# Attention masks on one Trainium2 core: the step between groups of 64 keys moved into idle rows of the query and key images, and the first mask product of a set cut from 128 keys to 64

## Chip, core and metric

The kernel runs on one core of one Trainium2 chip. The metric is the device time of one execution in microseconds; the number that counts is the median of several executions. The engines are named as in the profile: PE is TensorE (PEld are its weight loads), DVE is VectorE, ACT is ScalarE, POOL is GpSimd, SP is the SyncE queue that issues most of the transfers.

## What is computed

Two attention blocks read the same x (2048 rows of 512) and are mixed row by row by a gate. Block A works in four segments of 512 rows with 32 heads of 16: inside a segment it is causal softmax attention, and a memory of the earlier segments is added to it. Block B is full attention over all 2048 rows. Cut to what matters here:

```python
def _A_ref(x, wq, wk, wv, wo, beta):        # H=32 heads, Dh=16, N=4 segments, L=512
    ar = jnp.arange(L)
    mask = (ar[:, None] < ar[None, :]) * (-1e9)
    for s in range(N):
        qs, ks, vs = q[:, :, s], k[:, :, s], v[:, :, s]
        logits = jnp.einsum("bhqd,bhkd->bhqk", qs, ks) * scale + mask
        p = _softmax(logits, axis=-1)
        a_dot = jnp.einsum("bhqk,bhkd->bhqd", p, vs)
        a_mem = num / den                     # phi(q) against the memory M, z
        outs.append(g * a_mem + (1.0 - g) * a_dot)
        M, z = M + phi(k)^T v, z + sum(phi(k))
    return o @ wo

def _B_ref(x, wqkv, wo):                      # H=32, full attention over S=2048
    p = _softmax(jnp.einsum("bhqd,bhkd->bhqk", q, k) * (Dh ** -0.5))
    return o @ wo

g = sigmoid((x * gate_w).sum(-1))
return g * a + (1 - g) * b
```

The mask is the part that the change touches: a query sees the keys up to and including its own place in the segment.

## The kernel before

**Images.** Queries and keys of a unit are kept as images of 128 partitions: two halves of 64 rows (j = 0 and 1), one head in each half, and two heads behind one another (p = 0 and 1). Of the 64 rows of a half, 48 hold the 16 numbers of a head as high and low parts, in an order that makes one product over 64 rows the full-precision score. Rows 48 and 49 hold the negated row maximum on the query side (two parts, written by `m_rows`) and ones on the key side. Rows 50 to 63 are zero in all images: these are the idle rows. `load_qk` fetches an image from device memory; for a query image it writes rows 0 to 49 (the last two with zeros), for a key image rows 0 to 47. So what stands in rows 50 to 63 is written once, before the first unit, and stays. A's images are KA and QA (two buffers each), B's are KB and QB (three each).

**Units.** A unit is four heads times 512 queries. There are 32 of A (u = 0 to 31, causal, 512 keys) and 32 of B (u = 32 to 63, 2048 keys). After the projections the main loop runs k from 0 to 31; step k takes B's unit 32 + k in 32 groups (n = 0 to 31) and then A's unit k in 5 groups (n = 32 to 36). A group is laid down in PE's order by hand: `t_group` makes transposed scores of two heads in two PSUM banks and ACT turns them into exponentials; then come the maximum tasks that the table `plan` gives for this place; then `pvs` multiplies earlier exponentials with the values.

**Maxima.** The exponentials need the row maximum of every query beforehand. It is made one unit ahead, from a second score product that is not transposed (queries on partitions): `s_b` for B and `s_a` for A write into one of two buffers `SBK` of two banks each, and DVE reduces the buffer to a maximum. In step k the six calls of `s_a` for unit k + 1 stand at n = 32, 33, 34, 34, 35 and 36 (`ST_A`: the query blocks of 128 numbered 3, 3, 2, 2, then 1 and 0 with both p in one call). That stretch of a step, n = 32 to 36, is called the A stage below.

**The mask in `s_a`.** For query block i the score product covers the keys 0 to 128(i + 1). The last 128 keys of it are the diagonal block, on which a mask is accumulated in the same bank. It takes two more products for each half j, each over 64 rows in bf16: `crows[r, n2 - 1]` picks 64 of the 128 queries, and `cmask[r, n2 - 1]` holds, for each of them, -4e9 at the keys behind it. With n2 = 1, the first 64 queries, all 128 keys of the diagonal block are covered (keys 64 to 127 lie behind all of these queries); with n2 = 2, the last 64 queries, only the last 64 keys. The two halves j run beside each other on different rows of the array. So a set (one i and one p) has six products: two scores, two first mask products of 128 columns, two second ones of 64 columns; a unit has 8 sets, and 4 first products in each call for blocks 1 and 0, which hold two sets.

In the transposed scores of `t_group` the mask is applied later: POOL sets the entries behind the diagonal to zero after the exponential (`affine_select`).

**Before the main loop.** `constants` fills small tables on DVE and POOL in the first 14 us. `set_aux` copies 16 rows of constants (ones in the first two and zeros, or zeros alone) into rows 48 to 63 of an image, with two transfers that POOL issues; the list `ax` gives one image half p for each of A's value projections `v_job`, 12 entries for 16 jobs. QA is cleared by two DVE memsets instead.

Of the kernel before, what the change touches and what calls it, by code (L numbers as in the profile page):

```python
# [7 lines left out]
FT = mybir.dt.float32  # L8
# [4 lines left out]
OP = mybir.AluOpType  # L13
# [5 lines left out]
E = 16  # L19
SEQ = 2048  # L20
DM = 512
C = 512
# [3 lines left out]
MASK = -4.0e9  # L26
# [8 lines left out]
def gated_mix_kernel(ctx, tc, xt, wq, wk, wv, wo, beta, wqkv, wob, gate_w, out):  # L35
    nc = tc.nc
# [9 lines left out]
    QB = [P.tile([128, 2, C], FR, name=f"qb{s}") for s in range(3)]  # L46
    KA = [P.tile([128, 2, C], FR, name=f"ka{s}") for s in range(2)]
    QA = [P.tile([128, 2, C], FR, name=f"qa{s}") for s in range(2)]
# [3 lines left out]
    cmask = P.tile([128, 2, 128], BF, name="cmask")  # L52
    crows = P.tile([128, 2, 128], BF, name="crows")
# [13 lines left out]
    KB = [P.tile([128, 2, SEQ], FR, name="kb0")] + [t.rearrange("p a k t -> p a (k t)") for t in xh]  # L67

    proj = ExitStack()
    X = proj.enter_context(tc.tile_pool(name="proj", bufs=1))  # L70
# [5 lines left out]
    VS = [VB[0][:, 8 * i:8 * i + 8].rearrange("p (a t) h e -> p a (t h) e", a=2) for i in range(2)]  # L76
    bmask = X.tile([128, 8, E + 1], FT, name="bmask")
    aux = P.tile([E, 2, 64], FT, name="aux")
    MST = [[X.tile([128, 8, 32], FT, name=f"mst{i}{s}") for s in range(2)] for i in range(2)]

    TB = [PS.tile([128, C], FT, name=f"tb{i}") for i in range(2)]
# [26 lines left out]
    def rot(key, lst):  # L108
        i = cnt.get(key, 0)
        cnt[key] = i + 1  # L110
        return lst[i % len(lst)]
# [19 lines left out]
    def constants():  # L131
        nc.vector.memset(bmask, 1.0)
        nc.gpsimd.affine_select(out=bmask, in_=bmask, pattern=[[-E, 8], [0, E + 1]],
                                compare_op=OP.is_ge, fill=0.0, base=0, channel_multiplier=1)
        nc.gpsimd.affine_select(out=bmask, in_=bmask, pattern=[[E, 8], [0, E + 1]],
                                compare_op=OP.is_ge, fill=0.0, base=E - 1, channel_multiplier=-1)
        for a in MST:
            for m in a:
                nc.gpsimd.memset(m, 0.0)
        nc.vector.memset(PVB, 0.0)  # L140
        nc.gpsimd.memset(aux, 0.0)
        nc.gpsimd.memset(aux[0:2, 0], 1.0)

    def set_aux(t, a, eng=None):
        n = t.shape[1] // 64
        for j in range(2):
            (eng or nc.gpsimd).dma_start(t.bitcast(FT)[64 * j + 48:64 * j + 64].rearrange("r (n t) -> r n t", n=n),
                                         aux[:, a, None, :].to_broadcast([E, n, 64]))
# [44 lines left out]
    def load_beta():  # L193
        for g in range(4):
            nc.sync.dma_start(gh[:, g:g + 1], bass.AP(tensor=beta.tensor, offset=beta.offset + 8 * g,
                                                       ap=[[1, 8], [0, E], [1, 1]]))
        for qd in range(8):
            nc.sync.dma_start(nq[:, qd:qd + 1], bass.AP(tensor=beta.tensor, offset=beta.offset + 4 * qd,
                                                         ap=[[1, 4], [0, 32], [1, 1]]))
# [9 lines left out]
    def do_gate():  # L209
        e = X.tile([128, NT], FT, name="ge")  # L210
        nc.scalar.activation(e, sum_x(), AF.Exp, scale=-1.0)
        nc.vector.tensor_scalar(e, e, 1.0, None, op0=OP.add)
        nc.vector.reciprocal(gate, e)
# [28 lines left out]
    def load_wv(kd, k):  # L242
        src, c0 = wcols(kd, 2)
        WR[k] = raw_buf()
        nc.gpsimd.dma_start(WR[k], src[k * 128:(k + 1) * 128, c0:c0 + DM])
# [10 lines left out]
    def load_w(kd, g):  # L256
        WR[kd, g] = [load_w_raw(kd, g, w) for w in range(2)]

    def split_w(n, kd, g, ws=(0, 1)):
        for w in ws:  # L260
            split(WS[n][w][0], WS[n][w][1], WR[kd, g][w])
# [4 lines left out]
    def v_job(kd, tt):  # L266
        c, tl = divmod(tt, 4)
        b = misc()
        n = 0
        for xi, wi in TERMS:  # L270
            for k in range(4):
                lhs = (XH, XL)[xi][c][:, k, tl * 128:(tl + 1) * 128]
                nc.tensor.matmul(b, lhs, WV[wi][:, k, :], start=n == 0, stop=n == 11)  # L273
                n += 1
        if tl % 2 == 0:
            rot("vs", VS)
        vs = VS[(cnt["vs"] - 1) % 2]
        nc.scalar.activation(vs[:, tl % 2, :, :E], b.rearrange("p (h e) -> p h e", h=H), AF.Copy)
        if tl % 2:
            nc.sync.dma_start(VD[kd][tt * 128 - 128:(tt + 1) * 128].rearrange("(a t) g h e -> t a (g h e)", a=2),  # L280
                              vs.rearrange("p a h e -> p a (h e)"))
# [30 lines left out]
    def mem_state(g, c):  # L312
        return MST[c % 2][g % 2]

# [37 lines left out]
    def load_vm(g, c):  # L352
        PHI[g, "v", c] = X.tile([128, 4, 8, E + 1], FT, name="vm", bufs=2)
        v_src(PHI[g, "v", c], "A", g, c)
# [31 lines left out]
    def q_of(u):  # L386
        return QA[u % 2] if u < 32 else QB[u % 3]

    def k_of(u, p):
        return KA[u % 2][:, p] if u < 32 else KB[(u - 32) % 3][:, p]  # L390

    def load_q(u):
        kd, qd, c = UN[u]
        load_qk(q_of(u), kd, 0, qd, c)
# [5 lines left out]
    def load_kb(k, c=None):  # L400
        dst = KB[k % 3] if c is None else KB[k % 3][:, :, c * C:(c + 1) * C]
        load_qk(dst, "B", 1, k % 8, c)
# [16 lines left out]
    def pair_max(k):  # L419
        if k not in MX:  # L420
            MX[k] = W.tile([128, 2, 4, 4], FT, name="mx")
        return MX[k]

    def chain_of(u):

        return u + 1 if u else 0

    def s_a(u, i, p):
        mx = pair_max(chain_of(u))
        n = 128 * (i + 1)  # L430
        b = rot("s", SBK)
        todo_p = [(0, p)] if p is not None else [(0, 0), (256, 1)]
        for c0, p in todo_p:
            for n2 in range(3):
                for j in (1, 0):
                    r = slice(64 * j, 64 * j + 64)
                    if n2 == 0:
                        nc.tensor.matmul(b[:, j, c0:c0 + n], q_of(u)[r, p, i * 128:(i + 1) * 128], k_of(u, p)[r, :n],  # L438
                                         start=True, stop=False)
                    else:  # L440
                        w = 192 - 64 * n2
                        nc.tensor.matmul(b[:, j, c0 + n - w:c0 + n], crows[r, n2 - 1], cmask[r, n2 - 1, 128 - w:],  # L442
                                         start=False, stop=n2 == 2)
        m = mx[:, 0].rearrange("q (j p) i -> q j p i", j=2)
        if len(todo_p) == 1:
            nc.vector.tensor_reduce(m[:, :, p, i], b[:, :, :n], axis=AX.X, op=OP.max)  # L446
        else:
            nc.vector.tensor_reduce(m[:, :, :, i], b.rearrange("q j (p k) -> q j p k", p=2)[:, :, :, :n], axis=AX.X,
                                    op=OP.max)
# [194 lines left out]
    def todo(fn, *a):  # L644
        return lambda: fn(*a)
# [4 lines left out]
    def s_tasks(u):  # L650
        return [todo(s_a, u, *t) for t in ST_A] if u < 32 else [todo(s_b, u, *t) for t in ST_B]
# [14 lines left out]
    for k in range(2, 4):  # L666
        load_x3(k)
    constants()

    def split_next(c):  # L670
# [20 lines left out]
    for vs in VS:  # L691
        nc.gpsimd.memset(vs[:, :, :, E:E + 1], 1.0)
    load_w("A", 0)
    ax = [(t[:, p], int(n > 2)) for n, t in enumerate(KB[:1] + KA + QB) for p in range(2)]
    for t in QA:
        nc.vector.memset(t.bitcast(FT), 0.0)
    for tt in range(NT):
        v_job("A", tt)
        if tt == 2:
            split_w(0, "A", 0)  # L700
        if tt == 3:
            do_gate()
        if tt == 3:
            load_beta()
        if tt in (7, 9, 11):
            load_wv("B", (tt - 7) // 2)
        if tt == NT - 1:
            load_vm(0, 0)
            load_kb(0)
            load_q(32)  # L710
        if ax:
            set_aux(*ax.pop(0))
    first = s_tasks(32) + s_tasks(0)
    st33 = [todo(s_b, 33, *t) for t in sorted(ST_B, key=lambda t: t[2])]
    early = st33[:EARLY]
    fill = [todo(v_job, "B", tt) for tt in range(NT)]
# [20 lines left out]
    for blk in range(16):  # L737
# [9 lines left out]
        n = blk + 1 + (c == 2)  # L747
# [162 lines left out]
    for k in range(31):  # L910
        if k:
            spread([todo(s_b, 33 + k, *t) for t in (sorted(ST_B, key=lambda t: t[2]) if k == 1 else ST_B)],
                   [(k - 1, n) for n in range(2 * S_FIRST, 2 * NT)] + [(k, n) for n in range(2 * S_LAST)])
        else:
            spread(st33[EARLY:], sorted([(0, n) for n in range(2 * S_LAST)] + [(0, 2 * n) for n in range(4)]))
        for n, t in enumerate(ST_A):
            plan.setdefault((k, 2 * NT + n - (n > 2)), []).append(todo(s_a, k + 1, *t))
# [91 lines left out]
```

## Time and profile before

| | |
|---|---|
| median of 3 runs | 1962.55 us (1960.83 to 1966.76) |
| the profiled execution | 1963.14 us, its span from first to last instruction 1961.4 us |

Busy time by stretch of the span, in us, with the granted TensorE clock (1.00 is full speed):

| stretch | what runs | length | PE | DVE | ACT | POOL | clock |
|---|---|---|---|---|---|---|---|
| 0 to 37.7 | inputs, first projections | 37.70 | 29.47 | 27.23 | 17.70 | 18.90 | 1.00 |
| 37.7 to 283 | projections, A's memory | 245.30 | 244.18 | 118.75 | 78.39 | 25.76 | 0.99 |
| 283 to 330 | last projections, first maxima | 47.00 | 43.94 | 29.83 | 13.36 | 1.26 | 0.96 |
| 330 to 1889 | main loop with its 31 A stages | 1559.00 | 1553.32 | 1430.65 | 1280.57 | 209.25 | 1.00 |
| 1889 to 1961.4 | last A unit, output tail | 72.40 | 67.63 | 22.84 | 43.24 | 13.45 | 0.99 |

Reading: a row of the view of groups gives source line, engine, operation, the tile written and those read, shapes and count, then busy time in us and the mean of one in ns, then idle time before it. A row of the timeline is start, length, engine, line, with what ended a wait in brackets. A row of the chain of waits is start, length and the work that held the end at that moment; consecutive rows leave no gap, so such lengths can be added, while lengths in the timeline overlap (a product's recorded length includes its way through the array).

### The profile page before, as it was taken

The numbers are of one execution on the slowest core, as the hardware profiler recorded it, in microseconds if no ns is written. First come the engines' busy times: TensorE is split into PE (matmuls) and PEld (weight loads), VectorE is DVE, ScalarE is ACT, GpSimd is POOL, SyncE is SP. The second block draws the span as 40 slices with busy tenths as digits, with TensorE's granted clock in tenths as the row PEclk, the third lists the DMA queues.
The fourth block names the chain that finished last, engine by engine and source line by source line (L and its number), as shares of the span: only waits on it lengthen the run. The fifth ranks groups of instructions, "written<-read, shape, count | busy, mean of one in ns | idle before, by whom it ended". The sixth has DMA issues, their size and how long they took to land.

```text
span 1961.4 us, 43525 instructions
## 1 busy us (share of the span) xinstructions
PE 1938.5 (99%) x17485; PEld 942.3 (48%) x17485; DVE 1629.3 (83%) x1800; ACT 1433.3 (73%) x2699; POOL 268.6 (14%) x483
## 2 busy tenths in 40 slices
PE   8999999999999999999999999999999999999999
PEld 6887776444344444444444444444444444444445
DVE  6135765899999999999999999999999999999942
ACT  4233332688888888888888888888888888888884
POOL 4101000012120101111111111010101010101022
PEclk9999999999999999999999999999999999999999
DMA  7666656644443445343444443445444443434111
GB/s 221 170 195 195 194 187 179 154 98 114 97 115 90 108 90 107 82 111 81 115 87 114 87 114 86 113 86 114 87 107 95 107 95 88 101 88 107 48 50 58
DMA packets 163534, 222.23 MB, mean 113 GB/s; under 512 B 39788, under 2 KB 90428, under 8 KB 157572
## 3 DMA queue, kind: packets, MB, share of 16 engines
q1 hardware_dynamic: 159284, 211.41, 43.4%
q0 software_dynamic: 2992, 7.77, 2.1%
q8 instruction: 138, 2.26, 0.5%
q14 instruction: 64, 0.52, 0.1%
q10 hardware_dynamic: 1056, 0.26, 0.1%
HBM read 147.95 MB, written 68.16 MB: 110 GB/s over the span
## 4 chain that ended last, share of the span: by engine, by line
PE 95%; DVE 3%; ACT 1%; DMA 0%; SPq 0%; issue 0%; DVEq 0%; ACTq 0%
PE pvb L536 33%; PE tb L514 17%; PE sbk L460 12%; PE mb L514 9%; PE tb L290 4%; PE sbk L438 3%; PE tb L602 2%; PE mb L290 2%; PE sbk L273 1%; PE tb L273 1%; PE sbk L442 1%; PE pvb L290 1%; DVE mxb L462 1%; PE mb L602 1%; PE mb L273 1%; PE pvb L273 1%
## 5 line engine op out<-in xcount | busy, mean ns | idle before, releaser
L462 DVE TENSOR_REDUCE mxb<-sbk 128x2 f32<-128x1024 f32 x1024 | 1222.1, 1222 | 69.3 <-PE sbk L460 65.0
L520 ACT ACTIVATE raw<-tb 128x512 f32<-128x512 f32 x1555 | 887.6, 598 | 157.2 <-PE tb L514 81.7
L536 PE MATMUL pvb<-raw,vb 128*17 128x256 f32 (+1 forms) x8072 | 639.3, 388 | 0.0
L520 ACT ACTIVATE raw<-mb 128x512 f32<-128x512 f32 x782 | 467.9, 598 | 81.0 <-PE tb L514 38.3
L514 PE MATMUL tb<-qb,xh 64*128 64x512 f32 x872 | 331.1, 494 | 1.7 <-ACT raw L520 1.7
L536 PEld LDWEIGHTS pvb<-raw,vb 128*17 128x17 f32 x8072 | 134.4, 95 | 341.6 <-issue 336.5
L460 PE MATMUL sbk<-xh,qb 64*128 64x512 f32 x1344 | 281.7, 396 | 4.5 <-DMA xh<-dB 2.6
L514 PE MATMUL mb<-qb,xh 64*128 64x512 f32 x445 | 220.5, 495 | 0.0
L523 POOL TENSOR_SCALAR_AFFINE_SELECT raw<-raw 128x256 f32<-128x256 f32 (+1 forms) x320 | 115.5, 361 | 713.0 <-ACT raw L520 705.0
L514 PEld LDWEIGHTS tb<-qb,xh 64*128 64x128 f32 x872 | 124.5, 183 | 179.6 <-issue 90.1
L514 PE MATMUL tb<-qb,kb 64*128 64x512 f32 x470 | 179.4, 495 | 1.3 <-DVE st L300 0.8
L446 DVE TENSOR_REDUCE mx<-sbk 128x2 f32<-128x768 f32 (+1 forms) x128 | 136.7, 1090 | 25.2 <-PE sbk L442 19.2
L460 PE MATMUL sbk<-kb,qb 64*128 64x512 f32 x704 | 146.3, 398 | 0.0
L460 PEld LDWEIGHTS sbk<-xh,qb 64*128 64x128 f32 x1344 | 138.7, 186 | 9.0 <-DVE mxb L462 4.3
L514 PEld LDWEIGHTS mb<-qb,xh 64*128 64x128 f32 x445 | 81.3, 183 | 95.2 <-issue 50.4
L514 PEld LDWEIGHTS tb<-qb,kb 64*128 64x128 f32 x470 | 68.2, 183 | 100.1 <-issue 53.1
L514 PE MATMUL mb<-qb,kb 64*128 64x512 f32 x234 | 116.0, 496 | 0.0
L576 POOL TENSOR_TENSOR o<-o,d 128x512 f32<-128x512 f32 x31 | 39.8, 1283 | 548.9 <-DMA d<-rd 486.0
L536 PE MATMUL pvb<-raw,va 128*17 128x256 f32 (+2 forms) x1280 | 94.7, 384 | 0.8 <-ACT pvs L545 0.8
L438 PE MATMUL sbk<-ka,qa 64*128 64x256 f32 (+3 forms) x512 | 89.8, 358 | 0.3
L297 ACT ACTIVATE st<-tb 128x512 fp32r<-128x512 f32 x33 | 19.7, 598 | 84.4 <-DVE phi L296 49.1
L514 PE MATMUL tb<-qa,ka 64*128 64x512 f32 (+3 forms) x339 | 79.6, 372 | 0.0
(280 smaller groups left out, 1839.8 us busy)
## 6 DMA issues: line engine op xcount, KB each, us to landing
xh<-dB SPq DMA_DIRECT2D x38, 512.0 KB
vb<-vdB SPq DMA_DIRECT2D x16, 1088.0 KB
dB<-st SPq DMA_DIRECT2D x64, 256.0 KB
dA<-st SPq DMA_DIRECT2D x64, 256.0 KB
pd<-pvs SPq DMA_DIRECT2D x64, 256.0 KB
kb<-dB SPq DMA_DIRECT2D x22, 512.0 KB
xh<-dB SPq DMA_DIRECT2D x38, 256.0 KB
qb<-dB SPq DMA_DIRECT2D x64, 128.0 KB
```

The source lines that it names most:

```text
L273: nc.tensor.matmul(b, lhs, WV[wi][:, k, :], start=n == 0, stop=n == 11)
L290: nc.tensor.matmul(b, WS[ws][w][wi][:, k, :], (XH, XL)[xi][c][:, k, :], start=n == 0, stop=n == 11)
L438: nc.tensor.matmul(b[:, j, c0:c0 + n], q_of(u)[r, p, i * 128:(i + 1) * 128], k_of(u, p)[r, :n], start=True, stop=False)
L446: nc.vector.tensor_reduce(m[:, :, p, i], b[:, :, :n], axis=AX.X, op=OP.max)
L460: nc.tensor.matmul(b[:, j], q_of(u)[r, p, i * 128:(i + 1) * 128], k_of(u, p)[r, kc * C:(kc + 1) * C], start=True, stop=True)
L462: nc.vector.tensor_reduce(MXB[u][:, :, p, i, kc], b, axis=AX.X, op=OP.max)
L514: nc.tensor.matmul(bs[j][:, c0:c0 + w], k_of(u, h // 2)[r, 128 * it:128 * it + 128], q_of(u)[r, h // 2, q0:], start=True, stop=True)
L520: nc.scalar.activation(pt, bs[j], AF.Exp, scale=SCALE)
L523: nc.gpsimd.affine_select(out=m, in_=m, pattern=[[1, 128]] if n < 2 else [[0, 2], [1, 128]], compare_op=OP.is_ge, fill=0.0, base=0, channe ...
L536: nc.tensor.matmul(PVB[32 * h:32 * h + E + 1, q0 + lo:q0 + hi], vt[:, it, 4 * q + h, :], pt[:, lo:hi], start=it == 0 and lo == 0, stop=it ...
L576: nc.gpsimd.tensor_tensor(o, o, d, op=OP.mult)
L602: nc.tensor.matmul(b, (AT["oh"], AT["ol"])[oi][:, g, a], (AT["wh"], AT["wl"])[wi][:, g, a], start=n == 0, stop=n == 11)
```

## The change

A tile `steps` of 16 rows and 512 columns is made for each side. On the key side row r (from 2 on) holds -4e9 from key 64(r - 1) on and zero before, with ones in rows 0 and 1; on the query side row r holds 1 for the 64 queries of group r - 2 alone. Their product is -4e9 wherever the key's group of 64 lies behind the query's, and zero elsewhere. These rows are copied to rows 48 to 63 of KA and QA in place of what stood there, so every product of A's images, transposed or not, contains the mask between groups. The first mask product then only has to mask inside its own group: 64 columns at the first 64 keys of the diagonal block. The number of products stays. Three memsets and three `affine_select` are added on POOL in `constants`; the two DVE memsets of QA go; the list `ax` grows from 12 to 16 entries, with QB's ahead of KA's and QA's at the end.

```diff
+    steps = X.tile([E, 2, C], FT, name="steps")
...
         nc.gpsimd.memset(aux[0:2, 0], 1.0)
+        for a, v in ((0, MASK), (1, 1.0)):
+            s = steps[:, a].rearrange("r (b t) -> r b t", t=64)
+            nc.gpsimd.memset(s, v)
+            nc.gpsimd.affine_select(out=s, in_=s, pattern=[[1, 8], [0, 64]], compare_op=OP.is_ge, fill=0.0,
+                                    base=1 + a, channel_multiplier=-1)
+            if a:
+                nc.gpsimd.affine_select(out=s, in_=s, pattern=[[-1, 8], [0, 64]], compare_op=OP.is_ge, fill=0.0,
+                                        base=-2, channel_multiplier=1)
+        nc.gpsimd.memset(steps[0:2, 0], 1.0)
+
+    def set_steps(t, a):
+        for j in range(2):
+            nc.gpsimd.dma_start(t.bitcast(FT)[64 * j + 48:64 * j + 64], steps[:, a])
...
-                        w = 192 - 64 * n2
-                        nc.tensor.matmul(b[:, j, c0 + n - w:c0 + n], crows[r, n2 - 1], cmask[r, n2 - 1, 128 - w:],
-                                         start=False, stop=n2 == 2)
+                        w = slice(64 * n2 - 64, 64 * n2)
+                        nc.tensor.matmul(b[:, j, c0 + n - 128 + w.start:c0 + n - 128 + w.stop], crows[r, n2 - 1],
+                                         cmask[r, n2 - 1, w], start=False, stop=n2 == 2)
...
-    ax = [(t[:, p], int(n > 2)) for n, t in enumerate(KB[:1] + KA + QB) for p in range(2)]
-    for t in QA:
-        nc.vector.memset(t.bitcast(FT), 0.0)
+    ax = [todo(set_aux, t[:, p], int(n > 0)) for n, t in enumerate(KB[:1] + QB) for p in range(2)]
+    ax += [todo(set_steps, t[:, p], a) for a, ts in enumerate((KA, QA)) for t in ts for p in range(2)]
...
-            set_aux(*ax.pop(0))
+            ax.pop(0)()
```

## The prediction

> **What bounds the kernel now.** I read the page's totals and its chain of waits first, to learn which engine the time belongs to.
>
> ```profile
> span 1961.4 us, 43525 instructions
> PE 1938.5 (99%) x17485; PEld 942.3 (48%) x17485; DVE 1629.3 (83%) x1800; ACT 1433.3 (73%) x2699; POOL 268.6 (14%) x483
> PE 95%; DVE 3%; ACT 1%; DMA 0%; SPq 0%; issue 0%; DVEq 0%; ACTq 0%
> ```
>
> PE is busy 99% of the span and is 95% of the chain that ends last. A busy PE can still hide short waits, because a product's recorded length holds its way through the array. So I went to the place of the change, the A stage, in the chain of waits of one step (the one at 925 us; lengths there can be added).
>
> ```profile
> 928.32 0.17 PE sbk L442 x4
> ...
> 929.47 0.23 PE sbk L438 x2
> 929.70 0.10 PE sbk L442 x4
> ...
> 931.02 0.10 PE sbk L442 x4
> ...
> 931.57 0.10 PE sbk L442 x4
> ...
> 932.83 0.10 PE sbk L442 x4
> ...
> 933.13 0.10 PE sbk L442 x4
> ...
> 934.23 0.06 PE sbk L438 x2
> 934.28 0.10 PE sbk L442 x4
> ...
> 934.53 0.10 PE sbk L442 x4
> ```
>
> All eight sets of masks (L442 x4) are on the chain, and hardly anything that is not PE: in this stage time taken from PE is time taken from the end, until another engine's result comes too late. The mask products have these forms over the whole run:
>
> ```profile
> L442 PE MATMUL sbk<-cmask,crows 64*128 64x128 bf16 x512 | 61.5, 227 | 0.0
> L442 PE MATMUL sbk<-cmask,crows 64*128 64x64 bf16 x512 | 51.8, 189 | 0.0
> ```
>
> 512 first products of 128 columns, 512 second ones of 64. The halves j run beside each other, so they count as 256 pairs, 8 for each unit.
>
> **The change part by part.**
>
> *The shorter first product.* It loses 64 columns. What columns cost on the chain: scores of 512 columns take 0.23 us (929.47), of 128 columns 0.06 us (934.23); 0.17 us for 384 columns is 0.44 ns for one, so 64 are 0.028 us. This fits the masks: 128 and 64 columns are 192 x 0.44 = 0.085 us, and their 0.10 us leaves 0.015 us for both starts. Bounds: nothing, if something other than columns sets the distance from the first to the second product; 0.038 us, the difference of the two forms above (227 less 189 ns). I take 0.028, from work of the same stage. Rounded lengths allow 0.16 to 0.18 us for the 384 columns, 0.027 to 0.030 us for 64.
>
> In the first set the two halves run apart (0.17 us for four), each still first product, second product; the later half sets the end and has one first product of its own, so 0.028 us there too.
>
> *Where it is not gained.* Between the two sets of block 2 PE waits for a DVE reduction:
>
> ```profile
> 930.86 0.26 PE L442 MATMUL sbk<-cmask,crows 64*128 64x128 bf16 x4
> 931.13 0.19 PEld L438 LDWEIGHTS sbk<-ka,qa 64*128 64x128 f32 x2 [0.16 <-DVE mx L446]
> ```
>
> PEld's idle time there is 0.16 us and ends with the reduction that frees the score buffer. This reduction follows the masks of block 3's second set, so it moves earlier by two pairs, while PE would come earlier by three. The third pair only lengthens the wait. The view of what line 438 waits for says that this is so in nearly all steps:
>
> ```profile
>   DVE mx L446: 4.7, 30
> ```
>
> 30 waits, 4.7 us, one for each step but one. So 7 of 8 pairs count. The stage occurs 31 times (k = 0 to 30): 31 x 7 x 0.028 = 6.1 us. Unit 0's eight pairs run before the main loop, between reductions that follow on each other; up to 0.2 us, taken as nothing.
>
> *Does the earlier PE run into something later?* Two places have little room. The transposed scores of n = 34 use a bank that ACT frees:
>
> ```profile
> 929.56 1.09 ACT L520 ACTIVATE raw<-tb 128x512 f32<-128x512 f32 x2 [0.39 <-PE tb L514]
> 930.29 0.44 PE L514 MATMUL mb<-qa,ka 64*128 64x384 f32 x1
> 933.42 0.89 POOL L523 TENSOR_SCALAR_AFFINE_SELECT raw<-raw 128x256 f32<-128x256 f32 x2 [0.83 <-ACT raw L520]
> 934.56 1.06 PE L536 MATMUL pvb<-raw,va 128*17 128x384 f32 x16
> L520 ACT ACTIVATE raw<-tb 128x512 f32<-128x512 f32 x1555 | 887.6, 598 | 157.2 <-PE tb L514 81.7
> ```
>
> ACT's first of the two exponentials starts at 929.56 and takes 0.60 us, so the bank is free at 930.16, 0.13 us ahead of PE; between ACT's start and PE's product lies one pair (block 3's second set), and ACT itself follows PE, so the room shrinks by 0.028. The value product at n = 36 needs POOL's zeroing, which ends at 934.31, 0.25 us ahead of it; between the scores that feed POOL and this product lie four pairs, 0.11 us. Both still fit. The handover costs something too: in step 931 about 0.05 us from the end of DVE to the load. After the stage B's groups hang on each other, T product to exponential to T product, and start from the moved end; the 6.1 us are kept.
>
> *The image rows.* The score and T products have the same shapes with other numbers in rows that were streamed anyway: nothing. The work that hides a cost elsewhere is named for the rest:
>
> ```profile
> 13.36 0.14 POOL L142 MEMSET aux<- 2x64 f32 x1
> 16.01 2.49 POOL L173 TENSOR_TENSOR xl<-raw,xh 128x1024 fp32r<-128x1024 f32 x1 [2.51 <-ACT xh L171]
> 18.50 1.08 PE L290 MATMUL mb<-xl,ws 128*128 128x512 f32 x4
> 37.72 0.50 PE L273 MATMUL mb<-wv,xh 128*128 128x512 f32 x1 [0.70 <-DVE wv L233]
> L139 POOL MEMSET mst<- 128x256 f32 x4 | 1.1, 311 | 0.0
> L523 POOL TENSOR_SCALAR_AFFINE_SELECT raw<-raw 128x256 f32<-128x256 f32 x192 | 78.1, 407 | 76.0 <-ACT raw L520 68.0
> L523 POOL TENSOR_SCALAR_AFFINE_SELECT raw<-raw 128x128 f32<-128x128 f32 x128 | 37.4, 292 | 637.0 <-ACT raw L520 636.9
> L147 POOL DMA_DIRECT2D qb<-aux x12 | 6.3, 532 | 2.7 <-DMA ka<-aux 1.6 <-DMA raw<-in_B_wqkv_dram 0.6 <-DMA qb<-aux 0.3
> L696 DVE MEMSET qa<- x2: 912/912/912, 41.2 to 42.3; 128x1024 f32 x2
> ```
>
> In `constants` POOL gets two memsets of 512 elements, at most 0.62 us each (twice the 311 ns of 256), three selects of 512, about 0.64 each (292 ns for 128 and 407 for 256, so 115 for each further 128), and a small memset of 0.14: 3.3 us. POOL is idle from 13.50 to 16.01, 2.51 us. Queued behind is the low part of x for the second chunk; it would be some 0.8 us late, done near 19.3 instead of 18.50. PE reaches the first four products with low parts at 18.50 and needs POOL's half from the third on, some 0.5 us later. What remains, 0 to 0.4 us, falls into the 0.70 us for which PE waits for DVE at 37.72; without that cover it would be 0.4.
>
> Of the transfers, 8 more are issued on POOL (four entries of two), at 0.53 us each 4.3 us of POOL in the value projections, in the last four of 16 jobs, behind all of the weight loads of that loop. Nothing reads QA before the first maxima of A, far behind. Nothing on the path. Removing DVE's two memsets (0.91 us each, at 41 us, when PE runs alone on the path): nothing.
>
> *Sum:* 1961.4 - 6.1 = 1955.3 us of span. The profiled execution was 1.7 us longer than its span (1963.14), which gives 1957.0; it lay 0.6 us above the median, so 1962.55 - 6.1 = **1956.5 us** is predicted, 0.31% less.
>
> **Rule against the trace.** The rows: four masks in 0.10 us of chain. The Trainium skill, "TensorE: Matmul & The Clock Gate", section "Back-to-back issue gap", says that in a stream of weight loads and products the distance is set by both, about 81 ns per product at 128 columns. This is the rule that speaks against the change, as each mask product has its own load; the trace disagrees with its number, since both first and both second products with their loads fit into 100 ns. By the rule nothing would be saved, which is the second rival below.
>
> **Rivals.**
>
> *More than columns.* If the recorded lengths tell the price, 0.038 us, 31 x 7 x 0.038 = 8.2 us: 1954.3. For it: the forms, over 512 each. Against: the chain, where the four together have 0.10. Chance 0.12.
>
> *The distance does not shrink.* If the load of the second mask's weights sets it, nothing is gained: 1962.6. For it:
>
> ```profile
> L442 PEld LDWEIGHTS <-crows 64*128 64x128 bf16 x1024 | 32.0, 95 | 19.8 <-issue 9.0
> 931.41 0.12 PEld L442 LDWEIGHTS <-crows 64*128 64x128 bf16 x4
> ```
>
> a load is recorded with 95 ns, longer than 64 columns (28 ns). Against: four of them take 0.12 us together, so they start within 25 ns, long before the second product. Chance 0.08.
>
> *Taken back in the stage.* If POOL's zeroing (room 0.25 us) or the bank (0.13) already decides with its handover, up to four pairs are lost: 31 x 3 x 0.028 = 2.6 us remain, 1960.0. Chance 0.08.
>
> *Slower: the clock.* Before the main loop a stretch shows a halved clock:
>
> ```profile
> 315.00:318.40 3.40, 0.79 (x5) 0.52 (x4) 0.69 (x1) 0.88 (x2) 0.00 (x0) 1.00 0.59 160
> 318.40:321.80 3.40, 3.40 (x14) 2.36 (x12) 2.92 (x4) 0.00 (x0) 0.45 (x1) 0.50 0.56 203
> 330.00:1889.00 1559.00, 1553.32 (x15553) 657.67 (x15552) 1430.65 (x1468) 1280.57 (x2386) 209.25 (x384) 1.00 0.44 100
> ```
>
> 3.4 us at half speed cost 1.7 us. It follows 3.4 us in which PE worked 0.79 us. Less streaming in an A stage could bring it below the limit of the gate: from four such stretches on (6.1 / 1.7) the kernel is slower, with one in every stage it is 31 x 1.7 - 6.1 = 47 us slower (2009). Against: the clock is 1.00 over all 31 stages, and a stage loses 8 x 0.028 of 8 us. Chance 0.08, with every cause of a loss that I do not see.
>
> **How the numbers follow.** The forecast has 0.64. A change under 0.3% (5.9 us) cannot be told from none. The forecast lies 0.2 us beyond; its column price (0.027 to 0.030) spreads it over 5.9 to 6.5 us, runs scatter more: 0.41 of its 0.64 go to faster, 0.23 to the same. With the larger gain (0.12) faster has 0.53; with the two rivals of small or no gain same has 0.39; slower 0.08. The range, 1953.5 to 1963.0, holds the forecast, the rivals with less, and the larger gain, with a run's scatter; the slow clock lies outside.
>
> **What would show it.** Right: 1024 mask products of 64 columns near 190 to 200 ns; L442 x4 at 0.07 us instead of 0.10 in the chain, in seven sets; the wait of the load at L438 grown from 0.16 to 0.18 or 0.19 us; steps shorter by 0.19 us. Wrong: L442 x4 still 0.10; a load or product in the stage that now waits for ACT or POOL; a clock of 0.50 between 392 and 1889 us; PE waiting for POOL's low parts near 19 us and the wait at 37.72 grown rather than shrunk.

## The result and the profile after

| | before | changed |
|---|---|---|
| median of 7 runs each | 1962.63 us (1960.0 to 1966.76) | 1959.23 us (1956.4 to 1960.04) |
| ratio, with its 95% interval | | 0.9974 (0.9962 to 0.9986) |
| the same two again, 20 and 12 runs on another occasion | 1962.14 us | 1959.87 us, ratio 0.9986 (0.9977 to 0.9996) |
| the profiled execution and its span | 1963.14, 1961.4 us | 1956.4, 1954.7 us |

By the ratios the kernel is faster by 0.26% (5.1 us) on the first occasion and by 0.14% (2.7 us) on the second; the medians differ by 3.4 and 2.3 us. The forecast was 0.31% less, 1956.5 us. Both intervals lie below 1, but both gains are smaller than the 0.3% under which the prediction counted a change as none. The profiled executions differ by 6.7 us, which is treated below.

The page of the changed kernel, and the chain of waits of the same A stage (start, length, what held the end; line 452 is the score product of `s_a`, line 456 its mask products, line 528 the transposed scores):

```profile
span 1954.7 us, 43539 instructions
PE 1930.3 (99%) x17485; PEld 939.3 (48%) x17485; DVE 1629.9 (83%) x1798; ACT 1433.4 (73%) x2699; POOL 275.8 (14%) x497
```

```profile
925.39 0.43 PE tb L528 x2
925.82 0.23 PE sbk L452 x2
926.05 0.07 PE sbk L456 x4
...
927.34 0.07 PE sbk L456 x4
927.41 0.04 issue
927.45 0.44 PE sbk L452 x2
927.89 0.07 PE sbk L456 x4
...
929.12 0.07 PE sbk L456 x4
929.20 0.20 PE sbk L452 x2
929.40 0.07 PE sbk L456 x4
...
930.52 0.07 PE sbk L456 x4
930.60 0.14 PE sbk L452 x2
930.74 0.07 PE sbk L456 x4
...
931.80 0.42 PE mb L528
```

Each of the seven sets of masks shown holds the chain for 0.07 us where it was 0.10, and nothing between them became longer, but for the gap named "issue" ahead of block 2's second set: 0.04 us, where the kernel before had this:

```profile
927.62 0.43 PE tb L514
...
931.12 0.01 issue
...
935.62 0.42 PE mb L514
```

From the first product of n = 32 to the first of the next step the stage before takes 935.62 - 927.62 = 8.00 us. The changed one starts at 924.00 (a row of the same line ahead of those shown) and ends at 931.80: 7.80. Over the 31 stages of each trace, measured between the starts of these two products, the means are 8.008 and 7.823 us, 0.185 less. The groups by form have one form of mask product where there were two:

```profile
L456 PE MATMUL sbk<-cmask,crows 64*128 64x64 bf16 x1024 | 61.7, 195 | 0.0
```

The start is the other place that changed. The timeline of POOL, PE and DVE in the changed kernel (line 146 and following build the step rows, line 187 makes the low part of x, line 304 is a projection, line 196 begins the gate's sum over x, line 247 splits weights):

```profile
13.45 0.52 POOL L146 MEMSET steps<- 16x512 f32 x1
14.04 0.66 POOL L147 TENSOR_SCALAR_AFFINE_SELECT steps<-steps 16x512 f32<-16x512 f32 x1
14.64 0.52 POOL L146 MEMSET steps<- 16x512 f32 x1
15.23 1.11 POOL L147 TENSOR_SCALAR_AFFINE_SELECT steps<-steps 16x512 f32<-16x512 f32 x1
16.41 0.65 POOL L150 TENSOR_SCALAR_AFFINE_SELECT steps<-steps 16x512 f32<-16x512 f32 x1
17.02 0.51 POOL L152 MEMSET steps<- 2x512 f32 x1
17.51 2.34 POOL L187 TENSOR_TENSOR xl<-raw,xh 128x1024 fp32r<-128x1024 f32 x1
19.81 2.38 POOL L187 TENSOR_TENSOR xl<-vb,xh 128x1024 fp32r<-128x1024 f32 x1
```

```profile
17.47 0.63 PE L304 MATMUL mb<-xl,ws 128*128 128x512 f32 x2
19.90 0.73 PE L304 MATMUL mb<-xl,ws 128*128 128x512 f32 x2 [1.80 <-POOL xl L187]
...
26.03 1.20 PE L304 MATMUL sbk<-xl,ws 128*128 128x512 f32 x4 [0.77 <-DVE xl L187]
...
39.24 0.50 PE L287 MATMUL mb<-wv,xh 128*128 128x512 f32 x1 [0.71 <-DVE wv L247]
```

```profile
14.61 1.23 DVE L187 TENSOR_TENSOR xl<-raw,xh 128x1024 fp32r<-128x1024 f32 x1 [0.26 <-ACT xh L185]
16.44 0.69 DVE L314 TENSOR_TENSOR st<-tb,st 128x512 fp32r<-128x512 f32 x1 [0.61 <-ACT st L311]
17.05 5.43 DVE L196 TENSOR_SCALAR phi<-raw,gw 128x512 f32<-128x512 f32 x1
...
24.76 1.22 DVE L187 TENSOR_TENSOR xl<-vb,xh 128x1024 fp32r<-128x1024 f32 x1
```

POOL's subtraction starts at 17.51 instead of 16.01. PE waits 1.80 us for it, which it did not before. DVE's multiplication of line 196 is recorded with 5.43 us (0.71 for the same work before) and ends at 22.48, just behind POOL's second subtraction (22.19). DVE's next low part of x is late by that, PE waits another 0.77 us, and the wait at the first value projection ends at 39.24 instead of 37.72. It is as long as before, 0.71 us: PE and DVE are late together.

The kernel before has the same contest between DVE and POOL, in another order (line 173 makes the low part of x there, lines 182 and 184 are the gate's sum):

```profile
18.08 0.71 DVE L182 TENSOR_SCALAR phi<-raw,gw 128x512 f32<-128x512 f32 x1
18.83 4.36 DVE L184 SCALAR_TENSOR_TENSOR phi<-raw,gw,phi 128x512 f32<-128x512 f32 x3
23.11 1.22 DVE L173 TENSOR_TENSOR xl<-vb,xh 128x1024 fp32r<-128x1024 f32 x1
```

```profile
19.42 2.43 POOL L173 TENSOR_TENSOR xl<-vb,xh 128x1024 fp32r<-128x1024 f32 x1 [0.92 <-ACT xh L171]
```

There too one of DVE's operations is held, and the three of line 184 take 4.36 us where the same three take 2.33 in the changed kernel (from 22.52). But POOL pauses for 0.92 us between its two subtractions, and DVE gets two of the four operations of the gate's sum done before the second one ends at 21.85. In the changed kernel POOL does not pause, and all four end behind it. So DVE's next low part of x starts at 24.76 instead of 23.11, 1.65 us late: 0.34 us because POOL's second subtraction ends later, 1.31 us because more of DVE's work is left behind it.

### The profile page after: what moved, and what is told of

Same layout as the page of the kernel before. It is cut to its first block, busy times and chain, and to the rows that moved or that the text cites. A ratio compares the mean times of both kernels' runs of the same rounds, so it can differ in the third digit from the quotient of the medians.

```text
span 1954.7 us, 43539 instructions
## 1 busy us (share of the span) xinstructions
PE 1930.3 (99%) x17485; PEld 939.3 (48%) x17485; DVE 1629.9 (83%) x1798; ACT 1433.4 (73%) x2699; POOL 275.8 (14%) x497
## 4 chain that ended last, share of the span: by engine, by line
PE 95%; DVE 3%; ACT 1%; SPq 1%; DMA 1%; issue 0%; DVEq 0%; ACTq 0%
PE pvb L550 33%; PE tb L528 17%; PE sbk L474 12%; PE mb L528 9%; PE tb L304 4%; PE sbk L452 3%; PE tb L616 2%; PE mb L304 2%; PE sbk L287 1%; DVE mxb L476 1%; PE tb L287 1%; PE pvb L304 1%; PE mb L616 1%; PE sbk L456 1%; PE mb L287 1%; PE pvb L287 1%
```

## Experiments

Ten profiles are compared in one table. "Stage" is the mean of the 31 A stages as above; "distance" is the mean distance of the stages' first mask products (30 steps); "third projection" is the start of the third value projection; "halved" counts the stretches of 3.4 us at half the clock ahead of the first A stage (392 us).

| run | stage, us | distance, us | third projection, us | halved | wait of PE near 317 us |
|---|---|---|---|---|---|
| before | 8.008 | 49.685 | 41.78 | 2 | 2.6 |
| before again (e7) | 8.006 | 49.673 | 41.88 | 1 | 0.7 |
| changed | 7.823 | 49.513 | 43.30 | 1 | 0.5 |
| changed again (e5) | 7.825 | 49.535 | 43.87 | 3 | 0.5 |
| e1 steps later | 7.823 | 49.496 | 41.78 | 3 | 1.0 |
| e6 the same again | 7.818 | 49.533 | 41.47 | 2 | 1.9 |
| e2 build only | 8.009 | 49.695 | 43.77 | 3 | 0.9 |
| e3 wide first | 8.004 | 49.712 | 43.42 | 1 | 0.9 |
| e4 spread sets | 8.040 | 49.643 | 41.26 | 2 | 0.6 |
| e8 first 16 | 7.791 | 49.499 | 43.79 | 0 | 0.8 |

### e1: the step rows built later

```diff
     def constants():
...
         nc.gpsimd.memset(aux[0:2, 0], 1.0)
+
+    def make_steps():
         for a, v in ((0, MASK), (1, 1.0)):
...
+        if tt == 4:
+            make_steps()
         if ax:
             ax.pop(0)()
```

> The changed kernel, with the six POOL instructions that build the step rows moved out of the start and into the value projections (behind the fifth of A's 16), where POOL has little to do. Theory (the start is late because POOL's splitting of x stands behind these six, and DVE behind POOL): PE waits for POOL at 19 us no longer, the wait at the first value projection ends near 37.7 us again instead of 39.2, and the stages' distance stays 49.51 us. Whether the end moves by these 1.5 us is open between two theories: the wait of PE for a transfer near 317 us (2.6 us in the kernel before, 0.5 in the changed one) grows by the same amount and the time stays within 0.5 us of the changed kernel's 1959.2 us; or it does not, and the time is 1.5 us lower. Rival (the lateness comes from other things, such as the place of the new tile): the wait at 39.2 stays.

The ratio to the kernel before is 0.9964 (0.9951 to 0.9976), the median 1956.35 us. The timeline of POOL and PE at the start (lines 189 and 306 here are 187 and 304 of the changed kernel):

```profile
15.97 2.50 POOL L189 TENSOR_TENSOR xl<-raw,xh 128x1024 fp32r<-128x1024 f32 x1 [2.26 <-ACT xh L187]
18.76 2.41 POOL L189 TENSOR_TENSOR xl<-vb,xh 128x1024 fp32r<-128x1024 f32 x1 [0.28 <-ACT xh L187]
```

```profile
17.85 1.41 PE L306 MATMUL mb<-xl,ws 128*128 128x512 f32 x4
```

POOL starts its subtraction when ACT's part is there, PE's four low products take 1.41 us (1.08 in the kernel before) without the wait of 1.80, and the third value projection starts at 41.78 us, where it started in the kernel before. The stages are those of the changed kernel. So the six instructions made the start late; the place of the tile did not, nor did the eight added transfers, which this kernel has as well. Whether the end gains by it needed the direct comparison of e6.

### e2: the step rows built at the start and not used

```diff
+    steps = X.tile([E, 2, C], FT, name="steps")
...
         nc.gpsimd.memset(aux[0:2, 0], 1.0)
+        for a, v in ((0, MASK), (1, 1.0)):
...
+        nc.gpsimd.memset(steps[0:2, 0], 1.0)
```

> The kernel before, with the six POOL instructions added at the start and their result not used; images and masks as before. Theory: the start is late by 1.5 us (wait of PE for POOL near 18 us, first value projection released near 39.2 us), the stages' distance is that of before (49.68 us), and the wait near 317 us shrinks from 2.6 us to about 1 us, so that the end moves by less than 0.5 us. Rival (the lateness is paid in full): 1.5 us slower.

The ratio is 1.0010 (1.0000 to 1.0020): slower by 2 us, with an interval from nothing to 4. The start is late as in the changed kernel (third projection 43.77 us), with the same wait of PE:

```profile
20.34 0.73 PE L300 MATMUL mb<-xl,ws 128*128 128x512 f32 x2 [1.48 <-POOL xl L183]
```

and the stages are those of before, 8.009 us. The wait near 317 us is 0.9 us, as the theory had it, but the kernel before has 0.7 when it is profiled again (e7), so this says little. Of the two outcomes written down, the lateness paid in full fits better.

### e3: the first product with 128 columns on the new images

```diff
-                        w = slice(64 * n2 - 64, 64 * n2)
+                        w = slice(64 * n2 - 64, 128)
```

> The changed kernel, with the first mask product kept at 128 columns (the step between the groups of 64 is then masked twice). Theory (the gain is columns alone): first to second mask product 66 to 71 ns apart again instead of 39, stages 49.68 us apart as in the kernel before, time 5 us above the changed kernel. Rival (part of the gain, or a loss, comes from what stands in the image rows, for example in the transposed scores or the exponentials): the stages' distance differs from 49.68 us by more than 0.05.

1.0011 (1.0002 to 1.0020), the same as e2, which has the same late start and the same stages; against the changed kernel's two ratios it is 4.9 to 7.3 us more, where 5 were expected. The chain of waits of one stage:

```profile
927.45 0.42 PE tb L528
...
929.53 0.10 PE sbk L456 x4
...
930.85 0.10 PE sbk L456 x4
...
935.45 0.42 PE mb L528
```

0.10 us for a set again, and 935.45 - 927.45 = 8.00 us for the stage. With the step rows in all images and in every score, transposed or not, the stage is that of the kernel before. The gain in the stages is the 64 columns, and the image rows cost nothing.

### e4: the sets of masks spread over the groups

```diff
-            plan.setdefault((k, 2 * NT + n - (n > 2)), []).append(todo(s_a, k + 1, *t))
+            plan.setdefault((k, 2 * NT + min(n, 4)), []).append(todo(s_a, k + 1, *t))
```

> The kernel before, with the six calls of the maximum product placed at n = 32, 33, 34, 35, 36, 36 instead of 32, 33, 34, 34, 35, 36. Theory (the second set of block 2 waits about 0.17 us for DVE because it follows the first one at once, and this wait swallows one pair of the change): the wait disappears, steps are 0.15 to 0.2 us shorter, 5 us in all. Rival (the wait moves to the last calls, where then two stand at n = 36, or POOL's zeroing comes too late for the value product): a wait of PE for DVE or POOL at n = 36 of 0.1 us or more, steps unchanged or longer.

0.9994 (0.9984 to 1.0003): no difference that can be told. The wait for DVE is gone, and at n = 34 the value product waits for something else (timeline):

```profile
929.99 0.60 ACT L545 ACTIVATE pvs<-pvb 128x512 f32<-128x512 f32 x1
930.74 0.63 PE L536 MATMUL pvb<-raw,va 128*17 128x256 f32 x8 [0.16 <-ACT pvs L545]
```

It writes the bank that ACT copies out from 929.99 to 930.59, and this copy comes behind ACT's two exponentials. PE waits so in all 31 stages, 0.16 us each. In the kernel before the second set of block 2 stands between, and the copy is done in its shadow, 0.47 us before the value product starts at 931.60:

```profile
930.53 0.60 ACT L545 ACTIVATE pvs<-pvb 128x512 f32<-128x512 f32 x1
```

The stage became 8.040 us. Both theories missed: another wait of the same size came in place of the first, and not at n = 36.

### e5, e6, e7: the changed kernel, the later build and the kernel before again

No edits. Three more profiles, and the changed kernel and that of e1 timed on the same chip.

> The changed kernel once more, for a second profile and more times beside e6. Theory (the profiled time of 1956.4 us had only one stretch of halved clock and a short wait near 317 us, and these two change from execution to execution): the number of halved stretches and the wait near 317 us differ from the first profile, the stages' distance (49.51 us) and the start (first value projection released at 39.2 us) do not. Rival (they belong to the change): one halved stretch near 53 us and 0.5 us of wait again.

> The kernel of e1 once more on the same chip as the changed kernel. Theory (the lateness of the start is paid in full at the end): 1.5 us below the changed kernel. Rival (it is absorbed by the transfer near 317 us): the same time within 0.5 us.

> The kernel before once more, for a second profile. Theory: the wait near 317 us is not 2.6 us again but between 0.5 and 1 us as in the other four profiles, and the halved stretches differ in number or place; stages 49.69 us apart. Rival (both belong to the kernel before): 2.6 us and a halved stretch near 318 us again.

The changed kernel has 0.9986 (0.9977 to 0.9996), the kernel of e1 0.9976 (0.9966 to 0.9986): 2 us apart, and so were their first ratios (0.9974 and 0.9964). The medians on this occasion are 1.5 us apart, the means 2.3. The start of the changed kernel is not the same to the tenth, against the expectation: its third value projection began at 43.30 and at 43.87 us.

The mean granted clock of each run is on record, and the time goes with it. In the 27 runs of the kernel before that were timed beside e1 to e4, those with a clock of 0.999 took 1961.1 us in the mean, with 0.998 1962.4, with 0.997 1964.6 and with 0.996 1966.8. A straight line of time against clock, fitted to the runs of a kernel and those of the kernel before on the same occasion (its slope is 1.7 to 2.0 us for 0.001), gives an estimate of the differences at equal clock, with 95% intervals:

| | less the kernel before, at equal clock |
|---|---|
| changed (e5) | -2.4 us (interval -3.3 to -1.5) |
| steps later (e1; e6) | -5.4 (-6.7 to -4.1); -5.1 (-6.0 to -4.2) |
| build only (e2) | 2.2 (1.1 to 3.2) |
| wide first (e3) | 2.3 (1.4 to 3.1) |
| spread sets (e4) | 0.6 (-0.4 to 1.6) |

The changed kernel is 2.7 us (1.8 to 3.6) above that of e6 in the same way. So the late start costs 2.2 to 2.7 us of the time by three comparisons (e2, e3, and e5 against e6), and the shorter stages save 5.1 to 5.4.

The clock in the second profile of the changed kernel, and near 318 us in the second one of the kernel before and the first one of the changed kernel (the last three columns are granted clock, DMA share and GB/s):

```profile
52.30:59.10 6.80, 6.80 (x20) 5.59 (x20) 0.43 (x2) 0.18 (x1) 3.70 (x7) 0.50 0.96 237
345.90:349.20 3.30, 3.30 (x9) 2.57 (x8) 1.38 (x2) 0.00 (x0) 0.00 (x0) 0.50 0.75 246
```

```profile
318.40:321.80 3.40, 2.77 (x14) 1.99 (x13) 3.19 (x4) 0.00 (x0) 0.45 (x1) 1.00 0.63 201
```

```profile
318.40:321.80 3.40, 2.77 (x16) 1.83 (x15) 3.40 (x5) 0.00 (x0) 0.45 (x1) 1.00 0.57 198
```

The changed kernel had one halved stretch the first time and three the second; the kernel before two and then one. The wait near 317 us was 2.6 and then 0.7 us in the kernel before, 1.0 and then 1.9 in that of e1, and 0.5 both times in the changed kernel, where the expectation had it differ. So neither the halved stretches nor the 2.6 us belong to a kernel. The first pair of profiles happened to differ in both, in favour of the change: between PE's 1441st and 1489th product (309 to 322 us) the kernel before took 13.5 us and the changed one 10.7. That is 2.8 of the 6.7 us by which the two spans differ. Another 5.1 are the 30 distances between the stages and 0.2 the tail; the late start is 1.5 the other way (-2.8 - 5.1 - 0.2 + 1.5 is -6.6).

The lateness of the start can be followed through the profiles. Five build the step rows at the start, five do not. In the first five POOL's two subtractions follow each other without a pause, DVE's multiplication takes 4.84 to 5.44 us, and DVE's next low part of x starts 2.6 us behind POOL's second subtraction; in the others POOL pauses for 0.28 to 0.92 us between the two, and it is 1.3 to 2.0 us. From there to the first value projection DVE works on without a pause (gaps of at most 0.04 us), and it takes 14.3 to 14.6 us in all ten. So DVE sets the lateness of this projection, and not the 1.80 us for which PE waits for POOL. The third value projection starts at 43.63 us in the mean of the first five, at 41.63 in that of the others: 2.0 us. For the 1489th product, with 1.7 us taken off for each halved stretch that came before it, the means are 320.1 and 318.4: 1.7 us. The waits near 317 us take up 0.3 us of the lateness by these means, which is less than the profiles of one group differ among themselves (1.0 and 1.5 us); the theory that they take up all of it is wrong.

### e8: 16 columns in the first mask product

```diff
-                        w = slice(64 * n2 - 64, 64 * n2)
+                        w = slice(64 * n2 - 64, (64 * n2) if n2 == 2 else 16)
```

> The changed kernel with the first mask product cut to 16 columns, so that the keys 16 to 63 of the first group of a diagonal block are not masked in the maximum. Theory (columns alone, 0.42 ns each): first to second product 19 to 21 ns apart instead of 39, stages 0.14 us nearer (7 x 20 ns), 49.37 us. Rival (a product has a least distance, for its weights or its start, of 25 ns or more): no nearer than that, stages 49.41 us or more.

One execution, 1955.9 us. The groups by form, and the timeline of two sets:

```profile
L456 PE MATMUL sbk<-cmask,crows 64*128 64x64 bf16 x512 | 50.9, 186 | 0.0
L456 PE MATMUL sbk<-cmask,crows 64*128 64x16 bf16 x512 | 49.3, 180 | 0.0
```

```profile
930.38 0.23 PE L456 MATMUL sbk<-cmask,crows 64*128 64x16 bf16 x4
930.44 0.31 PE L452 MATMUL sbk<-ka,qa 64*128 64x128 f32 x2
930.59 0.23 PE L456 MATMUL sbk<-cmask,crows 64*128 64x16 bf16 x4
```

Four products take 0.23 us with a last one of 186 ns, so the second starts 0.04 us behind the first. Product by product the trace has 38 to 39 ns in the sets of 16 columns and the same with 64, against 66 to 71 with 128. The stages are 0.03 us shorter than with 64 columns, not 0.14. The rival was right: there is a least distance, and 64 columns already stand at it. Where the 0.03 us come from is not shown.

## Why the prediction was right, and where it was not

**The shorter first product.** Right, in place and nearly in size. 0.028 us for a pair was forecast from the price of a column; the distance of the two products went from 66 to 71 ns down to 39. The sum of 7 pairs, 0.196 us for a stage, measured 0.185; 31 of them are 5.7 us instead of 6.1, and the times at equal clock without the late start say 5.1 to 5.4. e3 shows that the columns are all of it.

**What the price rested on.** The straight line of columns holds from 128 to 64 and not on to 16 (e8). The rival that something else sets the distance is wrong at 128 columns and right for what lies between 64 and 16. The rival of recorded lengths (38 ns a pair) is wrong: the chain gave 0.03 us for a set, the distances 27 to 32 ns.

**The eighth pair.** Right that it is lost, wrong in the view that was to show it. The load's wait is recorded with 0.16 us as before; it is counted from the end of the load ahead of it, and these loads did not move against each other. The chain shows the growth: "issue" at this place from 0.01 to 0.04 us. Whether the place would yield a pair if DVE did not hold it is not shown: e4 moves the whole set away, and the value product then comes early enough to meet ACT's copy, which in the kernel before is done 0.47 us ahead of it.

**Later waits in the stage.** Right: POOL's zeroing and ACT's bank stayed ahead of PE, no load of the stage waits for another engine than before.

**The rows at the start.** This is the step that failed: "What remains, 0 to 0.4 us, falls into the 0.70 us for which PE waits for DVE at 37.72". Three things were wrong in it and in what leads to it. The six instructions take POOL from 13.45 to 17.51, 4.06 us instead of 3.3: the last memset covers two rows of 512, 0.51 us, and was put at the 0.14 of one with 64; one select took 1.11 us beside DVE's subtraction of 14.61 to 15.84, where its like took 0.66. PE came to the low products at 17.47 instead of 18.50, which differs between executions (18.62 in e5). And the cover was none: PE waits at 37.72 for DVE, and DVE itself was late, since its operation of line 196 did not finish before POOL's subtractions and three more stood behind it. A wait for an engine hides only what does not delay that engine. The cost is 1.7 to 2.0 us in the profiles and 2.2 to 2.7 us of the time at equal clock, instead of nothing.

The Trainium skill, "SBUF — State Buffer", section "SBUF: two separate sides", says that GpSimd and, in some of its operations, VectorE share a pair of ports under an exclusive lock, held for a whole instruction. The trace agrees at both places: DVE's 5.43 us end 0.3 us behind POOL's second subtraction, and POOL's select of 1.11 us ends 0.5 us behind DVE's subtraction.

**The sum.** 5.7 us of stages less 1.7 us of start are 4.0 us; the two ratios say 5.1 and 2.7, the times at equal clock 2.4. Without the late start, in the kernel of e1, 5.7 us stand against 7.1 and 4.7, at equal clock 5.4 and 5.1. The forecast of 6.1 us was near because its main term was right; it was not met because a cost put at nothing took a third of it or more. That the first ratio comes within 1 us of the forecast is in part luck: the terms give 4.0 us or less.

**The clock.** The slow rival did not occur: no stage ran at a lower clock. That halved stretches come and go between executions, from none to three of 1.7 us each, was not seen. In the 27 runs above the difference between a clock of 0.999 and 0.996 is 5.7 us, as much as the change saves in the stages.

**What stays open.** Why DVE's multiplication, which waited since 17.05, did not get its turn between POOL's two subtractions is not shown. The start of the third value projection is 1.5 us late in the first profile of the changed kernel and 2.0 in the mean of five, and it differs by 0.6 us within either group; this was not followed further. What sets the least distance of 38 to 39 ns (the load of 128 columns of weights or the start of a product) was not tried.

The kernel of e1 is the best of those measured that mask all keys: the same stages as the changed kernel and the start of the kernel before, 0.9964 and 0.9976 of the time before.

## What to carry to other kernels

Before a cost is put into the shadow of a wait, look whom the wait is for, and whether the added work delays that engine too; small constants on POOL are cheap only where nothing that DVE needs is queued behind them or runs beside them. A product accumulated into a bank on PE's path is worth shortening by its columns as long as the distance to the next one follows the columns; a run with far fewer columns shows where that ends. One profile on each side is not enough to explain a difference of 0.3%: take the distances inside the loop, which repeat to a few hundredths of a microsecond, and a second profile for everything that stands outside it.

## What was unexpected of the hardware

Two mask products on the same rows of the array started 38 to 39 ns apart with 64 as with 16 columns, against 66 to 71 with 128. Stretches of half the TensorE clock ahead of the A stages differ between executions of the same kernel, from one to three in the two profiles of the changed kernel. A DVE operation that takes 0.5 to 0.7 us elsewhere was held to 5.43 us by two POOL subtractions in a row, longer than either of them; a pause of 0.28 us or more between the two was enough for DVE to get in.
